# The gate's logits taken from TensorE's columns and given to GpSimd and VectorE

## The chip, the cores and the metric

The program runs on one core of a Trainium2 chip. A core has five engines with a program each, run in its own order: TensorE (matrix products; PE in the profile, its weight loads PEld), VectorE (DVE), ScalarE (ACT), GpSimd (POOL) and SyncE (SP), which here issues every DMA. An engine waits where an operand isn't ready; what stands behind the waiting instruction on that engine waits too. The metric is the device time of one execution in microseconds; lower is better.

## The reference

One input `x` of 2048 positions and 448 channels goes two ways, and a gate mixes the results:

```python
g = _sigmoid((x * gate_w).sum(-1, keepdims=True))
a = _A_ref(x, A_wqkv, A_wo)
b = _B_ref(x, B_w1, B_b1, B_w2, B_b2)
return g * a + (1 - g) * b
```

`_A_ref` makes q, k and v by one product `x @ wqkv`, lets every position look at 8 positions (itself and every second one before it, 16 heads of 28 channels), and multiplies by `wo`. `_B_ref` is a two-layer network, 448 to 1792 to 448, with the square of a relu between. Inputs and outputs are float32. The change concerns the first line: one number per position, the logit `z = sum over channels of x * gate_w`, whose sigmoid is `g`.

## The kernel before

**Products.** A float32 number is split into a high part of type `fp32r` and a low part, the rest, and a product is three: high by high, high by low, low by high. The high part is a ScalarE copy, the low part a VectorE subtraction, both in `split_full` (L113, L114). 448 channels are three full slices of 128 rows and one of 64. Nearly all products are written side by side (`side_by_side`, L187): two products of 64 rows each, in the upper and the lower half of the array, for two accumulators. An accumulator gets first one half of its rows, then the other; between the two, `turn` has one engine write to a spare element of it (L197: a VectorE memset of one element), so that the second half can't begin before the first is done.

**Chunks.** The positions come in four chunks of 512, each four tiles of 128. Of chunk 0, q is made slice by slice as the loads land (`qkv_first`, L258, whole-height products), then k and v in 36 and 42 pairs; chunks 1 to 3 are two calls of `qkv_two` each, for two tiles: 63 pairs, of which 24 begin q and k, 12 begin v, 18 end q and k, and 9 end v. Four x tiles of chunk c are split some microseconds before it starts; chunk 0's low parts (L659, L661, L114) are made at the very start, as its loads land. ScalarE moves a finished accumulator to SBUF (`qkv_evacuate`, L206), SyncE stores it to `q_d`, `k_d` or `v_d`.

**The gate.** The weights of q carry two more columns, `gate_w` twice, so q's accumulators have 450 columns, and their column 448 is the logit. A ScalarE copy of 128x1 (L214) puts it into `zt` after each of q's 16 tiles. `gates` makes the sigmoid of it at 126 µs.

**Order.** The program is one list, written in order of a model clock that counts TensorE's products: `when(t, ...)` and `at(dt, ...)` put a piece of work into the list when the model clock has come to a time, and each engine gets its instructions in the order of that list. `SPLIT_AT` has the times at which chunks are split. From chunk 2 on the attention (`qk_piece`, L334, and `av_piece`, L341) runs on GpSimd, each product of 128x896 followed by a VectorE reduction (L335, L349). GpSimd has nothing before that but a few memsets.

**Buffers.** Raw loads of x, of q's weights and of w1 share two buffers (`raw_tile`); a load waits until all readers of the tile before it have finished. The attention's products have four (`pp`), its logits two (`lg`).

SyncE's DMAs go into one queue each, in order; an instruction of SyncE that waits for a semaphore holds all DMAs behind it.

Of the kernel before, what the change touches and what calls it, by code (L numbers as in the profile page):

```python
# [7 lines left out]
F32 = mybir.dt.float32  # L8
F32R = mybir.dt.float32r
AF = mybir.ActivationFunctionType  # L10
ALU = mybir.AluOpType
AX = mybir.AxisListType

S, D, H, DH, W, F = 2048, 448, 16, 28, 8, 1792
P = 128
# [5 lines left out]
C = HG * DH  # L21
NF = F // P
CH = 512
NQ = D + 2
NP = 512


# [23 lines left out]
PP_BUFS = 4  # L51
# [5 lines left out]
def gated_mix_kernel(ctx: ExitStack, tc: tile.TileContext, xT, wqkv, w1, w2, wo, b1, b2, out):  # L57
    nc = tc.nc

    def f32(ap):  # L60
        return ap.bitcast(F32)
# [4 lines left out]
    k_d = tc.dram_tile([2, G, SP + HALO, C], F32, name="k_d")  # L66
    v_d = tc.dram_tile([2, G, SP + HALO, C], F32, name="v_d")
    x_d = tc.dram_tile([3, 4, P, 2, CH], F32, name="x_d")
    f_d = tc.dram_tile([2, NS, P, D], F32, name="f_d")


# [20 lines left out]
    smp = ctx.enter_context(tc.tile_pool(name="smp", bufs=2))  # L92
    prodp = ctx.enter_context(tc.tile_pool(name="prodp", bufs=1))
# [3 lines left out]
    zt, gt, g1t = zg[:, 0:2], zg[:, 2:4], zg[:, 4:6]  # L97
# [14 lines left out]
    def split_full(raw, hi, lo, soon=now):  # L112
        nc.scalar.activation(hi, raw, AF.Copy)  # L113
        soon(lambda: nc.vector.tensor_sub(lo, raw, f32(hi)))  # L114

    def split_x78(raw, x7, x8, soon=now):

        split_full(raw, x7, x8, soon)
# [32 lines left out]
    xcp = actx.enter_context(tc.tile_pool(name="phase_a_own", bufs=1, reuse_waits="tile"))  # L151
    wqh = ap.tile([P, 3, NP + 2 * D], F32R, name="wqh")
    wql = ap.tile([P, 3, NP + 2 * D], F32R, name="wql")

    w7h = ap.tile([P, NP + D], F32R, name="w7h")
    w7l = ap.tile([P, NP + D], F32R, name="w7l")
    ap.tile([P, 48], F32, name="pad_a")
# [3 lines left out]

    stage = {}

    def ncols(b):
        return NQ if b == 0 else D

    def block(b):

        o = (0, NP, NP + D)[b]
        return slice(o, o + ncols(b))  # L170

    class Acc:

# [26 lines left out]
    def qkv_evacuate(pt, c, tl, b):  # L200
        par, t = c // 2, (c % 2) * 4 + tl
        first = (b, t // 2) not in stage
        if first:
            stage[b, t // 2] = xap.tile([P, G, 2, C], F32, tag="stage", name=f"st{c}_{tl}_{b}", bufs=ST_BUFS)
        st = stage[b, t // 2]
        nc.scalar.activation(st[:, :, t % 2], pt[:, :D].rearrange("p (g c) -> p g c", g=G), AF.Copy)  # L206
        if not first:
            stage.pop((b, t // 2))
            t0 = t - t % 2
            dst, off = ((q_d, 0), (k_d, HALO), (v_d, HALO))[b]  # L210
            dd = dst[par, :, off:off + SP].rearrange("g (p s) c -> p g s c", s=NS)[:, :, t0:t0 + 2]
            nc.sync.dma_start(dd.rearrange("p g s c -> p g (s c)"), st.rearrange("p g s c -> p g (s c)"))
        if b == 0:
            nc.scalar.activation(zt[:, par, t:t + 1], pt[:, D:D + 1], AF.Copy)  # L214

    def full(x, acc, tl, b, ks=range(3)):
        sl, n = slice(tl * P, tl * P + P), block(b)
        r = []
        for k in ks:
            r += [(acc, x.h[k][:, sl], wqh[:, k, n]), (acc, x.h[k][:, sl], wql[:, k, n]),  # L220
                  (acc, x.l[k][:, sl], wqh[:, k, n])]
        return r

    def last(x, acc, tl, b):

        sl = slice(tl * P, tl * P + P)
        n = block(1) if b == 2 else slice(0, ncols(b))
        h, l = w7h[:, n], w7l[:, n]
        return [(acc, x.x7[:, sl], h), (acc, x.x7[:, sl], l), (acc, x.x8[:, sl], h)]

    def accs(c, b, tls, tags):
        return [Acc(t, f"qkv{c}_{tl}_{b}", ncols(b)) for t, tl in zip(tags, tls)]

    def run(c, todo, steps):

# [13 lines left out]
    def qkv_first(x):  # L249


        four = range(4)
        q = accs(0, 0, four, "bbbb")
        for k in range(3):
            for two in ((0, 1), (2, 3)):
                for j, prods in enumerate(zip(*(full(x, q[i], i, 0, (k,)) for i in two))):
                    for acc, a, w in prods:
                        nc.tensor.matmul(acc.pt[:, :NQ], a, w, start=k == j == 0, stop=False)  # L258
            advance(12 * MM448)
        for acc in q:  # L260
            acc.todo = 3
        k = accs(0, 1, four, "mmmm")
        t = [sum((last(x, a[i], i, b) for i in four), []) for b, a in ((0, q), (1, k))]
        f = [full(x, k[i], i, 1) for i in four]
        run(0, [t[0] + f[0] + f[1] + f[2] + f[3], t[1] + f[2] + f[3] + f[0] + f[1]],
            [(3, [(0, 0, q[0])], (k[0], k[0])),
             (12, [(0, i, q[i]) for i in (1, 2, 3)], (k[1], k[1])),
             (24, [], (k[0], k[2])), (33, [], (k[1], k[3])),
             (39, [(1, 0, k[0]), (1, 2, k[2])]), (48, [(1, 1, k[1]), (1, 3, k[3])])])
        v = accs(0, 2, four, "bbbb")  # L270
# [200 lines left out]
    def soon(fn):  # L471
        at(LO_DELAY, fn)

    def advance(dt):
        clock["pe"] += dt
        while due := [x for x in later if x[0] <= clock["pe"]]:
            item = min(due, key=lambda x: x[0])
            later.remove(item)
            item[1]()
        if not clock["on"]:  # L480
            clock["att"] = clock["pe"]
            return
# [12 lines left out]
    def raw_tile(name):  # L495
        return rawp.tile([P, 4, 512], F32, tag="raw", name=name)
# [134 lines left out]
    raws = [raw_tile("wqraw0")]  # L631
    rx = raw_tile("xraw0")
    for k in range(4):
        if k < 3:
            nc.sync.dma_start(raws[0][:, k, :NQ], wqkv[0, :, k])  # L635
        else:
            for b, rows in ((0, slice(0, 64)), (1, slice(64, P))):
                nc.sync.dma_start(raws[0][rows, k, :NQ], wqkv[b, rows, k])
        for cols in ((slice(0, 256), slice(256, CH)) if k == 0 else (slice(0, CH),)):
            nc.sync.dma_start(rx[:, k, cols], xT[0, :, k, cols])  # L640

    for b, tag in ((1, "k"), (2, "v")):
        raw = attp.tile([P, 3, D], F32, tag=tag, name=f"wqraw{b}")
# [4 lines left out]
    nc.sync.dma_start(raw7, wqkv[2, :, 3, :D])  # L648
    x = x_tiles(0, xap)
    for k in range(3):  # L650
        nc.scalar.activation(wqh[:, k, :NQ], raws[0][:, k, :NQ], AF.Copy)
        halves = (slice(0, 256), slice(256, CH))
        for i, cols in enumerate(halves):

            if k == i == 0:
                nc.vector.tensor_copy(x.h[k][:, cols], rx[:, k, cols])
            else:
                nc.scalar.activation(x.h[k][:, cols], rx[:, k, cols], AF.Copy)  # L658
        nc.vector.tensor_sub(wql[:, k, :NQ], raws[0][:, k, :NQ], f32(wqh[:, k, :NQ]))  # L659
        for cols in halves:  # L660
            nc.vector.tensor_sub(x.l[k][:, cols], rx[:, k, cols], f32(x.h[k][:, cols]))  # L661
    split_full(raws[0][:, 3, :NQ], w7h[:, :NQ], w7l[:, :NQ])
    split_x78(rx[:, 3], x.x7, x.x8)

    def wq_split(b, k):
        if k < 3:
            split_full(raws[b][:, k], wqh[:, k, block(b)], wql[:, k, block(b)])
        else:
            split_full(raw7, w7h[:, NP:], w7l[:, NP:])

    def when(t, fn, *args):
        later.append((t, lambda: fn(*args)))

    xs, xm = {0: x}, {}
    xraw = {1: x_load(1)}
# [30 lines left out]
        wq_split(1, k)  # L708
    for k in range(4):
        when(12000.0 + k * 900.0, wq_split, 2, k)  # L710
    for c, t in SPLIT_AT.items():
        when(t, x_begin, c)
        for k in range(4):
            when(t + k * 900.0, lambda c, k: x_split(xraw[c], xs[c], k), c, k)
        if c < 3:
            when(t + 4500.0, x_more, c + 1)
            when(t + 5000.0, lambda c: x_spill(c, xs[c]), c)
# [321 lines left out]
    c, x = ORDER[0], xm[3]  # L1039
# [8 lines left out]
    for g in range(2, 2 * NF):  # L1048
        i, f = g // (NF // 2), g % (NF // 2) * 2
        c = ORDER[i]  # L1050
# [118 lines left out]
```

## Time and profile before

| | |
|---|---|
| time, median of 3 runs | 415.12 µs (414.99 to 416.3) |
| profiled execution, span from the first to the last instruction | 412.7 µs |
| TensorE busy | 408.2 µs (99%) |
| VectorE, ScalarE, GpSimd busy | 255.7, 211.3, 268.5 µs |
| DMA moved | 73.76 MB, 179 GB/s |

The profile gives the span of the profiled execution; 2.4 µs lie between it and the median time, the part of a run before the first and after the last instruction. A row of the groups names line, engine, operation, output and inputs by the program's names, shapes, count, busy time and mean duration of one, then the engine's idle time ahead of them and what ended it. A row of the timeline has start, duration, and in brackets the idle time before. `64*128 64x448` is a product of 64 rows on 128 columns with 448 columns moved through.

### The profile page before, as it was taken

The numbers are of one execution on the slowest core, as the hardware profiler recorded it, in microseconds if no ns is written. First come the engines' busy times: TensorE is split into PE (matmuls) and PEld (weight loads), VectorE is DVE, ScalarE is ACT, GpSimd is POOL, SyncE is SP. The second block draws the span as 40 slices with busy tenths as digits, with TensorE's granted clock in tenths as the row PEclk, the third lists the DMA queues.
The fourth block names the chain that finished last, engine by engine and source line by source line (L and its number), as shares of the span: only waits on it lengthen the run. The fifth ranks groups of instructions, "written<-read, shape, count | busy, mean of one in ns | idle before, by whom it ended". The sixth has DMA issues, their size and how long they took to land.

```text
span 412.7 us, 9327 instructions
## 1 busy us (share of the span) xinstructions
PE 408.2 (99%) x3835; PEld 378.0 (92%) x3835; DVE 255.7 (62%) x404; ACT 211.3 (51%) x477; POOL 268.5 (65%) x167
## 2 busy tenths in 40 slices
PE   8999999999999999999999999999999999999997
PEld 7999999999999999888888888989898888888996
DVE  4520433276767766777656798879576677891354
ACT  4641656388765565444565535444653254346540
POOL 0000001955999999989989899999899977940000
DMA  7989999969362315555112649764146630168304
GB/s 226 380 324 326 268 393 299 335 213 311 101 235 104 128 42 218 209 184 152 29 58 95 228 160 270 197 146 149 27 163 186 229 129 2 45 177 132 96 0 180
DMA packets 65611, 73.76 MB, mean 179 GB/s; under 512 B 32352, under 2 KB 58528, under 8 KB 65184
## 3 DMA queue, kind: packets, MB, share of 16 engines
q1 hardware_dynamic: 65568, 73.16, 55.1%
q8 instruction: 30, 0.49, 0.5%
q14 instruction: 13, 0.11, 0.1%
HBM read 45.71 MB, written 28.25 MB: 179 GB/s over the span
## 4 chain that ended last, share of the span: by engine, by line
PE 97%; DMA 1%; SPq 0%; DVE 0%; ACT 0%; issue 0%
PE b L187 33%; PE h L187 32%; PE qkv L187 23%; PE a L187 7%; PE qkv L258 1%; DMA xraw<-xT 1%; PE a L943 1%; PE last L943 0%; SPq L640 0%; SPq L635 0%; DVE bt L822 0%; ACT x L658 0%; PE last L935 0%; PE a L935 0%
## 5 line engine op out<-in xcount | busy, mean ns | idle before, releaser
L334 POOL TENSOR_TENSOR qk<-q,k 128x896 f32<-128x896 f32 x64 | 135.1, 2137 | 84.8 <-DMA k<-k_d 76.4
L341 POOL TENSOR_TENSOR av<-lg,v 128x896 f32<-128x896 f32 x64 | 119.4, 1961 | 6.3 <-DVE lg L335 5.8
L187 PE MATMUL qkv<-wqh,x 64*128 64x448 f32 (+1 forms) x528 | 89.1, 361 | 0.0
L615 DVE TENSOR_TENSOR h<-h,h 128x512 fp32r<-128x512 f32 x56 | 38.4, 688 | 65.9 <-ACT h L618 65.5
L187 PEld LDWEIGHTS qkv<-wqh,x 64*128 64x128 f32 x528 | 72.2, 184 | 0.8
L187 PE MATMUL qkv<-wql,x 64*128 64x448 f32 (+1 forms) x264 | 72.2, 360 | 0.0
L187 PE MATMUL b<-w2ah,h 64*128 64x448 f32 x448 | 68.5, 359 | 0.0
L187 PE MATMUL b<-w2bh,h 64*128 64x448 f32 x448 | 67.8, 360 | 0.0
L335 DVE TENSOR_REDUCE lg<-qk 128x32 f32<-128x896 f32 x64 | 67.0, 1074 | 0.0
L349 DVE TENSOR_REDUCE o<-av 128x112 f32<-128x896 f32 x64 | 66.4, 1070 | 0.1
L616 ACT ACTIVATE h<-h,b1z 128x512 f32<-128x512 f32 x56 | 36.7, 655 | 43.6 <-PE h L187 43.6
L187 PEld LDWEIGHTS b<-w2ah,h 64*128 64x128 f32 x448 | 46.9, 184 | 2.8
L187 PEld LDWEIGHTS b<-w2bh,h 64*128 64x128 f32 x448 | 45.3, 184 | 3.2 <-ACT h L567 0.3
L187 PEld LDWEIGHTS qkv<-wql,x 64*128 64x128 f32 x264 | 44.5, 184 | 0.4
L187 PE MATMUL b<-w2al,h 64*128 64x448 f32 x224 | 44.3, 358 | 0.0
L187 PE MATMUL b<-w2bl,h 64*128 64x448 f32 x224 | 43.2, 358 | 0.0
L206 ACT ACTIVATE st<-qkv 128x448 f32<-128x448 f32 x48 | 24.3, 546 | 34.8 <-PE qkv L187 26.9
L617 ACT ACTIVATE h<-h 128x512 fp32r<-128x512 f32 x56 | 33.5, 598 | 1.7
L618 ACT ACTIVATE h<-h 128x512 f32<-128x512 f32 x56 | 33.3, 594 | 0.0
L187 PE MATMUL h<-x,w1h 64*128 64x512 f32 x168 | 32.8, 386 | 0.0
L567 ACT ACTIVATE h<-h 128x4 fp32r<-128x4 f32 (+1 forms) x35 | 7.2, 207 | 43.1 <-PE b L187 43.0
L187 PE MATMUL h<-x2b,w1h 64*128 64x512 f32 x168 | 28.2, 386 | 0.0
(145 smaller groups left out, 728.7 us busy)
## 6 DMA issues: line engine op xcount, KB each, us to landing
k<-k_d SPq DMA_DIRECT2D x8, 840.0 KB, 6.4
v<-v_d SPq DMA_DIRECT2D x8, 840.0 KB, 4.8
x_d<-x SPq DMA_DIRECT2D x11, 512.0 KB, 6.6
q_d<-st SPq DMA_DIRECT2D x8, 448.0 KB, 4.1
k_d<-st SPq DMA_DIRECT2D x8, 448.0 KB, 4.6
v_d<-st SPq DMA_DIRECT2D x8, 448.0 KB, 5.9
w1raw<-w SPq DMA_DIRECT2D x4, 896.0 KB, 9.2
q<-q_d SPq DMA_DIRECT2D x8, 448.0 KB, 3.6
```

What stands on the lines that cost most here:

```text
L187: nc.tensor.matmul(acc.pt[:, :acc.n], a[rows], w[rows], start=acc.todo == acc.all, stop=acc.todo == 1)
L206: nc.scalar.activation(st[:, :, t % 2], pt[:, :D].rearrange("p (g c) -> p g c", g=G), AF.Copy)
L258: nc.tensor.matmul(acc.pt[:, :NQ], a, w, start=k == j == 0, stop=False)
L334: nc.gpsimd.tensor_mul(pr, q[:, s:s + 1].to_broadcast([P, W, C]), k[:, s:s + W])
L335: pending.append(lambda: nc.vector.tensor_reduce(lg[:, s], pr.rearrange("p w (h d) -> p w h d", h=HG), axis=AX.X, op=ALU.add))
L341: nc.gpsimd.tensor_mul(pr.rearrange("p (h d) w -> p w h d", h=HG), lg[:, s][:, :, :, None].to_broadcast([P, W, HG, DH]), v[:, s:s + W].rea ...
L349: nc.vector.tensor_reduce(o[:, g * C:(g + 1) * C], pr, axis=AX.X, op=ALU.add)
L567: nc.scalar.activation(ap, f32(ap), AF.Copy)
L615: nc.vector.tensor_sub(hl, pt, f32(hh))
L616: ops += [lambda pt=pt, r=r: nc.scalar.activation(pt, pt, AF.Relu, bias=b1t[:, f + r:f + r + 1]), lambda pt=pt, hh=hh: nc.scalar.activatio ...
L617: lambda pt=pt, hh=hh: nc.scalar.activation(hh, pt, AF.Square),
L618: lambda pt=pt, r=r, low=low: (nc.scalar.activation(pt, pt, AF.Square), at(delays[r], low))]
```

## The change

`ncols` goes: q's accumulators have 448 columns like k's and v's, and the 16 ScalarE copies of L214 go. The load of the weights still brings the two gate columns. New are:

```diff
-        wqh[:, k, :NQ] ... wql[:, k, :NQ] ... acc.pt[:, :NQ]
+        wqh[:, k, :D]  ... wql[:, k, :D]  ... acc.pt[:, :D]
-        if b == 0:
-            nc.scalar.activation(zt[:, par, t:t + 1], pt[:, D:D + 1], AF.Copy)
...
+    zs = smp.tile([P, 3, NZ], F32, tag="lg", name="zs")
+    zu = xcp.tile([P, CH], F32, tag="zu", name="zu")
+    zm = prodp.tile([P, W * C], F32, tag="pp", name="zm", bufs=PP_BUFS)[:, :CH]
+    zpart, zall, gw = zs[:, 0], zs[:, 1], zs[:, 2, 0:4]
+    nc.gpsimd.tensor_copy(gw[:, 0:3], raws[0][:, 0:3, D:D + 1].rearrange("p k n -> p (k n)"))
+    nc.gpsimd.tensor_copy(gw[0:64, 3:4], raws[0][0:64, 3, D:D + 1])
+
+    def z_products(raw):
+        for k in range(4):
+            r = slice(0, P if k < 3 else 64)
+            out = zm if k else zu
+            nc.gpsimd.tensor_mul(out[r], raw[r, k], gw[r, k:k + 1].to_broadcast([r.stop, CH]))
+            if k:
+                nc.gpsimd.tensor_add(zu[r], zu[r], zm[r])
+
+    def z_sums(c):
+        nc.vector.transpose(zu, zu)
+        nc.vector.tensor_reduce(
+            zpart.rearrange("p (b c t) -> p c t b", b=4, c=4)[:, c],
+            zu.rearrange("p (t b r) -> p t b r", t=4, b=4), axis=AX.X, op=ALU.add)
+
+    def z_move():
+        nc.sync.dma_start(z_d, zpart)
+        for b in range(4):
+            nc.sync.dma_start(
+                zall[b * 32:b * 32 + 32].rearrange("p (a n) -> p a n", a=4),
+                z_d[:, b * 16:b * 16 + 16].rearrange("(a c) n -> c a n", a=4))
+
+    def z_last():
+        nc.vector.tensor_reduce(
+            zt.rearrange("p q s -> p (q s)"), zall.rearrange("p (a n) -> p n a", a=4), axis=AX.X, op=ALU.add)
...
+    z_products(rx)
+    for c, t in enumerate((16500.0, 27000.0, 40000.0, 54500.0)):
+        when(t, z_sums, c)
+        if c < 3:
+            when(t + (500.0, 500.0, 5500.0)[c], lambda c: z_products(xraw[c + 1]), c)
+    when(59500.0, z_move)
+    when(67500.0, z_last)
```

For each chunk `z_products` has GpSimd multiply the raw x of a slice, channels on partitions and positions along the row, by the gate's weights and add up the slices: four products and three sums, 128x512 or 64x512, in one chain over `zu`. `z_sums` has VectorE transpose 32x32 blocks of `zu` in place, so that positions lie on partitions, and add up 32 channels. One tile `zu` serves all chunks, so the products of a chunk wait for the sums of the one before. Each of four groups of 32 partitions then has a part of each sum: `z_move` stores them to DRAM and reads them back in four DMAs with a group's parts beside each other, and `z_last` adds the four.

Four facts on the order of the engines. On VectorE, the sums of chunk 0 stand behind the last low part of the weights of v and ahead of the low parts of x of chunk 1 and the memsets that turn v's accumulators of chunk 0; the sums of chunk 3 stand ahead of the low part of x slice 2 and of the memset that turns the first accumulators of chunk 2; `z_last` stands ahead of the memsets that turn those of chunk 2's second half. On SyncE, `z_move` stands behind the first load of the attention's v and ahead of the stores of chunk 2. On GpSimd, the configuration instruction that the program has ahead of the first tensor_tensor stood behind the memsets; it now stands between the copies of the gate's weights and the first product.

More of the change, by code (lines that the diff above doesn't have):

```diff
@@ L24 @@
 NQ = D + 2
+NZ = 64
 NP = 512
@@ L68, in gated_mix_kernel @@
     x_d = tc.dram_tile([3, 4, P, 2, CH], F32, name="x_d")
+    z_d = tc.dram_tile([P, NZ], F32, name="z_d")
     f_d = tc.dram_tile([2, NS, P, D], F32, name="f_d")
@@ L162, in gated_mix_kernel @@
     stage = {}
-    def ncols(b):
-        return NQ if b == 0 else D
     def block(b):
         o = (0, NP, NP + D)[b]
-        return slice(o, o + ncols(b))
+        return slice(o, o + D)
     class Acc:
@@ L226, in last @@
         sl = slice(tl * P, tl * P + P)
-        n = block(1) if b == 2 else slice(0, ncols(b))
+        n = block(1) if b == 2 else slice(0, D)
         h, l = w7h[:, n], w7l[:, n]
@@ L231, in accs @@
     def accs(c, b, tls, tags):
-        return [Acc(t, f"qkv{c}_{tl}_{b}", ncols(b)) for t, tl in zip(tags, tls)]
+        return [Acc(t, f"qkv{c}_{tl}_{b}", D) for t, tl in zip(tags, tls)]
     def run(c, todo, steps):
@@ L257, in qkv_first @@
                     for acc, a, w in prods:
-                        nc.tensor.matmul(acc.pt[:, :NQ], a, w, start=k == j == 0, stop=False)
+                        nc.tensor.matmul(acc.pt[:, :D], a, w, start=k == j == 0, stop=False)
             advance(12 * MM448)
@@ L650, in gated_mix_kernel @@
     for k in range(3):
-        nc.scalar.activation(wqh[:, k, :NQ], raws[0][:, k, :NQ], AF.Copy)
+        nc.scalar.activation(wqh[:, k, :D], raws[0][:, k, :D], AF.Copy)
         halves = (slice(0, 256), slice(256, CH))
@@ L658, in gated_mix_kernel @@
                 nc.scalar.activation(x.h[k][:, cols], rx[:, k, cols], AF.Copy)
-        nc.vector.tensor_sub(wql[:, k, :NQ], raws[0][:, k, :NQ], f32(wqh[:, k, :NQ]))
+        nc.vector.tensor_sub(wql[:, k, :D], raws[0][:, k, :D], f32(wqh[:, k, :D]))
         for cols in halves:
             nc.vector.tensor_sub(x.l[k][:, cols], rx[:, k, cols], f32(x.h[k][:, cols]))
-    split_full(raws[0][:, 3, :NQ], w7h[:, :NQ], w7l[:, :NQ])
+    split_full(raws[0][:, 3, :D], w7h[:, :D], w7l[:, :D])
     split_x78(rx[:, 3], x.x7, x.x8)
+    zs = smp.tile([P, 3, NZ], F32, tag="lg", name="zs")
[25 more added lines that the diff above has]
+            zt.rearrange("p q s -> p (q s)"), zall.rearrange("p (a n) -> p n a", a=4), axis=AX.X, op=ALU.add)
     def wq_split(b, k):
```

## The prediction

> **What bounds the kernel now.** I read the page's busy shares and slices first, then the chain that ended last, then the groups by shape.
>
> ```profile
> span 412.7 us, 9327 instructions
> PE 408.2 (99%) x3835; PEld 378.0 (92%) x3835; DVE 255.7 (62%) x404; ACT 211.3 (51%) x477; POOL 268.5 (65%) x167
> ...
> POOL 0000001955999999989989899999899977940000
> DMA  7989999969362315555112649764146630168304
> ...
> PE 97%; DMA 1%; SPq 0%; DVE 0%; ACT 0%; issue 0%
> ```
>
> TensorE is busy 99% of the span and makes 97% of the chain that ended last: what TensorE does less is gained, and what makes it wait is lost, whole. GpSimd is empty for the first 70 µs, just where the new work goes; the DMA engines are full there (9 in most of the first eight slices).
>
> **The gain: narrower products.**
>
> ```profile
> L187 PE MATMUL qkv<-wqh,x 64*128 64x448 f32 x384 | 81.0, 359 | 0.0
> L187 PE MATMUL qkv<-wqh,x 64*128 64x450 f32 x144 | 44.1, 364 | 0.0
> ```
>
> ```profile
> 51.02 0.39 PE L187 MATMUL qkv<-wqh,x 64*128 64x448 f32 x2
> ...
> 51.25 0.53 PE L187 MATMUL qkv<-wqh,x 64*128 64x450 f32 x2
> ...
> 53.42 0.47 PE L187 MATMUL qkv<-wqh,x 64*128 64x448 f32 x2
> ...
> 53.73 0.45 PE L187 MATMUL qkv<-wqh,x 64*128 64x450 f32 x2
> ```
>
> The means differ by 5 ns. The pace shows more: in one stretch of pairs, from 51.02 to 53.42 the row half with 448 columns starts 12 products in 2.40 µs, 200 ns each; from 51.25 to 53.73 the half with 450 takes 2.48, 206.7 ns. Two columns cost 6.7 ns. The 24 pairs at the start of each of six half-chunks go at q's pace: 6 x 24 x 6.7 ns = 0.96 µs. Bounds: 0.2 (where only one half is slow, the other may set the pace in part) and 1.0; I take 0.9, since these 24 pairs come as two runs with q in the same half. The whole-height products of chunk 0 are paced by loads and splits: nothing. The 16 small copies of L214 go from ScalarE, which is idle half of the span, and no product waits for them: nothing.
>
> **The new work on GpSimd.** 28 products and sums, two small copies.
>
> ```profile
> L334 POOL TENSOR_TENSOR qk<-q,k 128x896 f32<-128x896 f32 x64 | 135.1, 2137 | 84.8 <-DMA k<-k_d 76.4 <-DVE lg L335 5.4 <-DVE o L349 2.3
> L387 POOL TENSOR_TENSOR lg<-lg,sm 128x256 f32<-128x256 f32 x8 | 5.1, 636 | 2.3 <-ACT h L618 2.3
> L349 DVE TENSOR_REDUCE o<-av 128x112 f32<-128x896 f32 x64 | 66.4, 1070 | 0.1
> L352 DVE STREAM_TRANSPOSE o<-o 128x448 f32<-128x448 f32 x16 | 10.2, 638 | 0.3
> L114 DVE TENSOR_TENSOR x<-xraw,x 128x512 fp32r<-128x512 f32 x13 | 8.4, 690 | 14.1 <-ACT x L113 14.1
> ```
>
> Between 256 elements (636 ns) and 896 (2137) lies 512 at 636 + 256 x 2.345 = 1236 ns. A chunk's seven are one chain over `zu`: 8.7 µs; four chunks 34.6 µs, which the idle 69.8 µs can hold. VectorE's sums: transposition 638 x 512/448 = 730, reduction 1070 x 512/896 = 610, with the hand-over 1.4 µs a chunk. So the amount fits; what counts is who stands behind a late step.
>
> **When the first chain can begin.**
>
> ```profile
> 0.74 1.28 ACT L651 ACT_TABLE_LOAD   x1 [0.74 <-PEq L1161]
> ```
>
> ```profile
> wqraw<-wqkv SPq DMA_DIRECT2D x2, 112.5 KB, 5.5
> ```
>
> ```profile
> 4.03 1.20 SPq L638 DMA_DIRECT2D wqraw<-wqkv  x2
> ```
>
> The second copy of the gate's weights waits for the first half of slice 3, issued at 4.03 and landing 5.5 µs later (rows two and three): 9.6. Then comes the configuration instruction. Before, it ran at 1.3 with GpSimd's first product at 71.2, so its price doesn't show. Its nearest rows: ScalarE's table load, 1.28 µs, and, if code comes through the same full queues, a transfer of that moment, 5.5 µs. I take 5.5: a table is loaded ahead of any traffic, this comes amid it. The first product starts at about 15.2.
>
> [...]
>
> **Who shares with whom.** While the chain of chunk 0 runs, VectorE makes low parts with two SBUF operands:
>
> ```profile
> 16.59 0.63 DVE L114 TENSOR_TENSOR wql<-wqraw,wqh 128x448 fp32r<-128x448 f32 x1 [2.99 <-ACT wqh L113]
> 17.32 0.09 DVE L197 MEMSET qkv<- 1x1 f32 x2
> 17.41 1.16 DVE L114 TENSOR_TENSOR wql<-wqraw,wqh 128x448 fp32r<-128x448 f32 x2
> 19.12 0.09 DVE L197 MEMSET qkv<- 1x1 f32 x2 [0.55 <-PE qkv L187]
> 19.21 0.62 DVE L114 TENSOR_TENSOR w7l<-wqraw,w7h 128x448 fp32r<-128x448 f32 x1
> 24.23 1.93 DVE L114 TENSOR_TENSOR x<-xraw,x 128x512 fp32r<-128x512 f32 x3 [4.40 <-ACT x L113]
> 25.52 0.06 DVE L197 MEMSET qkv<- 1x1 f32 x2
> ...
> 27.52 0.09 DVE L197 MEMSET qkv<- 1x1 f32 x2 [0.75 <-PE qkv L187]
> ```
>
> ```profile
> 71.19 12.58 POOL L334 TENSOR_TENSOR qk<-q,k 128x896 f32<-128x896 f32 x6 [69.80 <-DMA k<-k_d]
> ```
>
> ```profile
> L335 DVE TENSOR_REDUCE lg<-qk 128x32 f32<-128x896 f32 x64 | 67.0, 1074 | 0.0
> ...
> L513 ACT ACTIVATE copy<-w1raw 128x448 f32<-128x448 f32 x8 | 4.4, 548 | 2.0 <-DVE w1l L518 1.1 <-DVE w17l L518 0.8
> ```
>
> No such subtraction ever runs beside a GpSimd product in this trace: those of L114 are over before its first product at 71.19, and from there each VectorE subtraction has a PSUM operand (L518 from `copy`, L615 from `h`). So the price is open: nothing, or turns, where each subtraction waits for the product under way (up to 1.24 µs) and the next product for it (0.62 to 0.69). For nothing speaks that L335, with one SBUF operand, takes 1.07 µs beside GpSimd and without it; but it is of another kind. For turns speaks that every subtraction after 71 µs comes with a ScalarE copy of its operand to PSUM (L513, 548 ns), work that no number needs if two SBUF operands cost nothing there. I take turns, at three to one.
>
> [...]
>
> **The sum, stage by stage.** Chain 0 starts at 15.2, needs 8.7, and gives way to four subtractions (16.59 to 19.83, 4 x 0.62 = 2.5): it ends at 26.4. VectorE, in its order, now does chunk 0's sums (27.8), and only then what it did from 24.23 on. By then chain 1 is free to run, so: subtraction 0.69, product 1.24, subtraction 0.69, memset 0.1: 30.5. Product, subtraction, product, subtraction (3.9), memset: 34.4. These memsets turn v's accumulators; when TensorE needs them shows in its rows:
>
> ```profile
> 27.23 0.43 PE L187 MATMUL qkv<-wqh,x 64*128 64x448 f32 x2
> ...
> 63.39 0.36 PE L187 MATMUL qkv<-wqh,x 64*128 64x450 f32 x1
> ...
> 76.15 0.37 PE L187 MATMUL qkv<-wqh,x 64*128 64x450 f32 x1
> ```
>
> v's second half starts at 27.23 (after 24 of its 42 pairs), the other two tiles 9 pairs later, 29.0. TensorE waits 3.3 µs for the first and 5.4 in all for the second. Slack covered these steps, 1.6 and 1.4 µs (25.58 to 27.23, 27.61 to 29.03); without it TensorE stays late.
>
> Later sums: chain 1 ends about 39 and its sums at 40.4, ahead of a need at 38.1 + 5.4. Chain 2 ends at 49, its sums stand behind work of 45.1 + 5.4. Chain 3 waits for x of chunk 3:
>
> ```profile
> xraw<-xT SPq DMA_DIRECT2D x1, 1024.0 KB, 7.0
> ```
>
> ```profile
> 58.34 2.54 DVE L114 TENSOR_TENSOR x<-xraw,x 128x512 fp32r<-128x512 f32 x4 [5.84 <-ACT x L113]
> 60.24 0.06 DVE L197 MEMSET qkv<- 1x1 f32 x2
> ```
>
> ```profile
> 65.47 0.32 SPq L315 DMA_DIRECT2D v<-v_d  x1
> ```
>
> ```profile
> 56.20:81.70 25.50, 25.50 (x255) 24.73 (x254) 8.02 (x25) 13.74 (x30) 10.51 (x6) 1.00 1.00 334
> ```
>
> ```profile
> o_d<-o SPq DMA_DIRECT2D x16, 224.0 KB, 2.2
> ...
> ot<-o_d SPq DMA_DIRECT2D x16, 32.0 KB, 2.6
> ```
>
> Its load, issued at 46.2, lands at 53.2; the chain then takes 8.7 and two turns (1.4) to 63.3, sums 64.7, one subtraction and a memset 65.5. TensorE needs that at 63.39: 2.1 late in the old timing. The move: its store is queued behind v's load of 840 KB, issued at 65.47, itself behind k's, which lands at 71.1 (the row of GpSimd above); at the 334 GB/s of that stretch (last column of the row by stretches) v lands at 73.7. SyncE waits for the store, then issues four loads (0.4 each); they land 2.6 µs later (32 KB of `ot`), z_last ends about 78.5, the need is 76.15: 2.4 late. Both are counted against TensorE's old time: a TensorE 5.4 late, with the full DMA queues draining during its wait, meets both. They add nothing; without the first stall they would be the bound. GpSimd's attention starts at 71 or later, long after the chains; SyncE's stores of chunk 2 wait up to 6 µs behind the move, and ScalarE needs their buffers at 78.6 or later.
>
> Sum: + 5.4 - 0.9 = + 4.5 µs: a span of 417.2, and with the same 2.4 around it 419.6. The page gives no time of that execution beside its span; I take it to stand at the median.
>
> **The rivals.**
> - The configuration is short, 1.3 µs, with turns. The chain starts at 11.0 and meets chunk 0's own low parts: k's weights of slices 1 and 2 come about 0.8 and 1.9 late, then the memset at 19.12 comes at 24.1 for a need at 20.6; 3.5 lost in all, x's low parts then are in time. 415.1 + 3.5 - 0.9 = 417.7. Against it: the rows of loads at that moment.
> - No turns. The chain ends at 23.9, sums 25.3, the memset 26.8 for a need at 27.23: nothing lost there. Then z_move's 2.4 decides, with 0.7 of chain 3 (61.9 + 1.4 + 0.8 for 63.39) inside it: + 2.4 - 0.9, 416.6. For it: every VectorE row beside GpSimd is unslowed.
> - On the other side: the whole path of the logits is hidden, 415.1 - 0.9 = 414.2. One condition decides, that z's five DMAs don't queue behind v: if the store lands in the 2.2 µs of an `o_d` store, at 68, z_last is done by 73, before 76.15. It needs no turns as well. Against it: in the rows of the full stretch each load lands in order, 5 to 7 µs after issue.
> - VectorE gets its turn only when the chain ends: every low part behind 23.9 instead of 17.2, then again 8.7 µs of chain 1 ahead of x's low parts: 27.8 after the sums, 36.5 after chain 1, 39.3 for a need at 29.0, 10.3 lost: 424.5.
>
> **How the numbers follow.** Forecast 419.6: 0.53. Short configuration, 417.7: 0.13. No turns, 416.6: 0.18. Hidden: 0.05. No turn at all for VectorE, or longer configuration amid the traffic: 0.11. A measurement tells 0.3%, 1.25 µs, from no change. Faster by more than that: 0.02. Within it (up to 416.4): most of the hidden case and two fifths of the no-turns case, 0.11. Slower: 0.87. The range runs from 416.2 to 422.6: the lower end takes in the no-turns case, the upper a chain 3 µs later; the likeliest case alone has 418.3 (turns half as long) to 421.
>
> **What would show it.** In the changed profile: q's pairs at 200 ns; GpSimd's first product not before 15, with no row in the gap; VectorE's L114 rows beside it over 1 µs or started late, at gaps ended by GpSimd; a wait of TensorE near 29 to 34 on a VectorE memset, about 5 µs together, and none near 63 to 82. It is wrong if the chain begins by 11, if subtractions beside products start at once, or if TensorE's waits stand at z_last instead.

## The result and the profile after

The changed kernel takes 418.89 µs, median of 6 runs (418.25 to 423.62), beside 415.0 µs before on the same chip (414.19 to 416.3): a ratio of 1.0119, 95% interval 1.0082 to 1.0156. The profiled run took 418.62 µs with a span of 416.8, where before has a span of 412.7. In the changed file the line numbers have moved: L116 makes low parts, L186 is the side-by-side product, L196 the memset that turns an accumulator, L674 GpSimd's products, L676 its sums, L680 and L681 VectorE's transposition and sum.

The page of after:

```profile
span 416.8 us, 9352 instructions
...
PE 409.2 (98%) x3835; PEld 365.3 (88%) x3835; DVE 271.6 (65%) x413; ACT 210.7 (51%) x461; POOL 304.7 (73%) x197
...
POOL 1878152863999999989989999999989977940000
```

TensorE's busy time is hardly changed, and less than the span by more than before. GpSimd now works in the first seven slices. TensorE's waits up to 90 µs in after, each at the product that it ends at (timeline: start, duration, in brackets the wait and what ended it; a smaller loss near 94.5 follows below):

```profile
14.43 0.67 PE L186 MATMUL qkv<-w7h,x 64*128 64x448 f32 x4 [1.02 <-DVE x L116]
18.83 0.47 PE L186 MATMUL qkv<-wql,x 64*128 64x448 f32 x2 [0.50 <-DVE wql L116]
32.30 0.47 PE L186 MATMUL qkv<-wqh,x 64*128 64x448 f32 x2 [0.80 <-DVE qkv L196]
67.54 0.47 PE L186 MATMUL qkv<-wqh,x 64*128 64x448 f32 x2 [0.76 <-DVE qkv L196]
```

Before, TensorE has no wait in this stretch. All the waits are for VectorE, none for GpSimd: GpSimd acts through VectorE. To put sizes on it I take the stages of TensorE, from the start of one group of pairs to the next, worked out from the starts of its products in each trace. For all kernels of this study, in µs:

```
                    chunk 0   chunk 1   chunk 2 (a)  chunk 2 (b)  chunk 3 (a)   span
before               18.12     25.39      12.76        12.76        12.87      412.7
after                21.48     25.20      13.64        12.60        13.00      416.8
e1 narrow only       18.12     25.20      12.60        12.60        12.68      412.4
e2 memsets           19.55     25.20      14.35        12.60        12.69      414.9
e3 late chain 0      19.21     25.87      17.03        13.24        12.68      418.8
e4 tail moved        24.08     25.20      12.60        12.60        12.68      418.3
e5 both moves        19.20     25.87      12.60        12.60        12.68      414.9
e6 one operand       18.12     25.20      18.81        12.60        12.68      418.2
e7 on VectorE        18.12     25.20      12.60        12.60        12.67      412.0
e8 e6 and e4         18.12     25.20      12.60        12.60        12.67      412.4
```

Against the undisturbed stages (row e1) the changed kernel loses 3.36 µs in chunk 0, 1.04 in the first half of chunk 2 and 0.32 in the first half of chunk 3, 4.72 in all. Before is 0.70 longer than row e1 in these stages, so the difference is 4.02, of 4.1 between the spans. The stages leave out where the pairs begin, which moves from execution to execution: 12.4 to 13.2 µs in these ten traces, 12.71 in before and 13.20 in e1. That is why e1's span is only 0.3 below before's; spans that lie a few tenths apart should not be compared.

**The start.** GpSimd and VectorE in after, the same stretch (start, duration):

```profile
9.60 0.18 POOL L667 COPY zs<-wqraw 64x1 f32<-64x1 f32 x1 [1.33 <-DMA xraw<-xT]
9.82 1.22 POOL L674 TENSOR_TENSOR zu<-xraw,zs 128x512 f32<-128x512 f32 x1
...
13.91 1.37 POOL L674 TENSOR_TENSOR zm<-xraw,zs 128x512 f32<-128x512 f32 x1
15.36 1.56 POOL L676 TENSOR_TENSOR zu<-zu,zm 128x512 f32<-128x512 f32 x1
...
24.60 1.04 POOL L674 TENSOR_TENSOR zm<-xraw,zs 128x512 f32<-128x512 f32 x1
25.72 1.31 POOL L676 TENSOR_TENSOR zu<-zu,zm 128x512 f32<-128x512 f32 x1
```

```profile
12.62 1.76 DVE L116 TENSOR_TENSOR x<-xraw,x 128x512 fp32r<-128x512 f32 x1
14.30 6.68 DVE L116 TENSOR_TENSOR wql<-wqraw,wqh 128x448 fp32r<-128x448 f32 x5
...
20.91 0.61 DVE L116 TENSOR_TENSOR wql<-wqraw,wqh 128x448 fp32r<-128x448 f32 x1
...
26.48 4.24 DVE L116 TENSOR_TENSOR x<-xraw,x 128x512 fp32r<-128x512 f32 x3 [3.02 <-ACT x L115]
...
30.65 1.52 DVE L116 TENSOR_TENSOR x<-xraw,x 128x512 fp32r<-128x512 f32 x1
```

The first product stands 0.04 µs behind the copy. From then on five subtractions of 128x448 take 6.68 µs, 1.34 each on average: by single instructions 1.46, 1.72, 1.46 and 1.71 beside the chain, and 0.64 for the fifth, which starts behind the chain's end at 19.92. The one at 20.91, with GpSimd idle too, takes 0.61. GpSimd is slowed less: a product of 1.04 alone takes up to 1.37, a sum of 1.31 up to 1.62. The stage of chunk 0 has three groups of pairs, with 12, 36 and 42: they start at 12.74, 16.55 and 24.75 and the next stage at 34.22, so they lose 1.30, 0.99 and 1.07 µs against 12 x 0.210, 36 x 0.200 and 42 x 0.200 in row e1.

**The tail.** VectorE in after near 66, then SyncE and VectorE near 75:

```profile
65.38 0.71 DVE L680 STREAM_TRANSPOSE zu<-zu 128x512 f32<-128x512 f32 x1 [1.18 <-POOL zu L676]
66.12 0.69 DVE L681 TENSOR_REDUCE zs<-zu 128x16 f32<-128x512 f32 x1
66.73 1.32 DVE L116 TENSOR_TENSOR x<-xraw,x 128x512 fp32r<-128x512 f32 x2
67.40 0.71 DVE L196 MEMSET qkv<- 1x1 f32 x5
```

```profile
69.38 0.33 SPq L687 DMA_DIRECT2D z_d<-zs  x1
76.70 1.75 SPq L689 DMA_DIRECT2D zs<-z_d  x4
...
80.51 2.61 SPq L523 DMA_DIRECT2D w1raw<-w  x2
```

```profile
79.74 0.27 DVE L695 TENSOR_REDUCE zg<-zs 128x16 f32<-128x64 f32 x1 [5.70 <-DMA zs<-z_d]
```

VectorE stands 1.18 µs before chunk 3's transposition, and the memset behind it, which TensorE needed at 66.6, comes at 67.40. SyncE stands 6.9 µs for the store of the logits; z_last ends at 80.01, in time for the memsets behind it (needed at 80.26), but the loads of w1 behind it are issued at 80.51 (71.19 before), and the chain that ended last runs from that load (to 87.12) by ScalarE and VectorE to a memset at 94.81; TensorE's next pair starts behind it at 94.94, 0.2 µs late.

### The profile page after: what moved, and what is told of

It is laid out like the page before. It is cut to its first block, busy times and chain, and to the rows that moved or that the text cites. A ratio compares the mean times of both kernels' runs of the same rounds, so it can differ in the third digit from the quotient of the medians.

```text
span 416.8 us, 9352 instructions
## 1 busy us (share of the span) xinstructions
PE 409.2 (98%) x3835; PEld 365.3 (88%) x3835; DVE 271.6 (65%) x413; ACT 210.7 (51%) x461; POOL 304.7 (73%) x197
## 4 chain that ended last, share of the span: by engine, by line
PE 84%; DMA 8%; DVE 3%; issue 2%; SPq 1%; ACT 1%; DVEq 0%
PE b L186 32%; PE h L186 32%; PE qkv L186 12%; PE a L186 7%; DMA v_d<-st 2%; DMA z_d<-zs 2%; DMA w1raw<-w 2%; DMA wqraw<-wqkv 1%; DVE wql L116 1%; DVE x L116 1%; DMA xraw<-xT 1%; PE a L983 1%; DVE lg L332 1%; ACT st L205 0%; SPq L211 0%
## 5 line engine op out<-in xcount | busy, mean ns | idle before, releaser
L612 DVE TENSOR_TENSOR h<-h,h 128x512 fp32r<-128x512 f32 x56 | 38.4, 688 | 66.9 <-ACT h L615 66.6
L186 PE MATMUL qkv<-wqh,x 64*128 64x448 f32 x528 | 78.6, 360 | 1.6 <-DVE qkv L196 1.6
L186 PE MATMUL b<-w2ah,h 64*128 64x448 f32 x448 | 66.3, 359 | 0.0
L186 PE MATMUL b<-w2bh,h 64*128 64x448 f32 x448 | 66.2, 360 | 0.0
L186 PEld LDWEIGHTS qkv<-wqh,x 64*128 64x128 f32 x528 | 49.4, 184 | 6.2 <-DVE qkv L196 2.7
L186 PE MATMUL qkv<-wql,x 64*128 64x448 f32 x264 | 48.1, 361 | 0.5 <-DVE wql L116 0.5
L186 PEld LDWEIGHTS b<-w2bh,h 64*128 64x128 f32 x448 | 42.0, 184 | 3.8 <-ACT h L564 0.3
L186 PEld LDWEIGHTS b<-w2ah,h 64*128 64x128 f32 x448 | 41.9, 184 | 3.7
L186 PE MATMUL b<-w2bl,h 64*128 64x448 f32 x224 | 40.7, 358 | 0.0
L186 PE MATMUL b<-w2al,h 64*128 64x448 f32 x224 | 40.5, 358 | 0.0
L186 PE MATMUL h<-x,w1h 64*128 64x512 f32 x168 | 28.2, 386 | 0.0
L186 PE MATMUL h<-x0b,w1h 64*128 64x512 f32 x168 | 28.1, 386 | 0.0
L186 PE MATMUL h<-x1b,w1h 64*128 64x512 f32 x168 | 28.1, 386 | 0.0
```

The costliest lines, as they stand in the source:

```text
L186: nc.tensor.matmul(acc.pt[:, :acc.n], a[rows], w[rows], start=acc.todo == acc.all, stop=acc.todo == 1)
L612: nc.vector.tensor_sub(hl, pt, f32(hh))
```

## The experiments

My theory after the result: VectorE's subtractions with two operands in SBUF are slowed beside GpSimd's work (chunk 0), and the places of the late sums and of the move in the queues cost the rest; the narrower products by themselves gain something under 1 µs. Rivals: the narrow products gain nothing; any work of GpSimd slows VectorE; the tail's waits are covered anyway.

**e1_narrow: the gain alone.**

```diff
-    zs = smp.tile([P, 3, NZ], F32, tag="lg", name="zs")
...
+    nc.gpsimd.memset(zt, 0.0)
...
-    z_products(rx)
...
-    when(59500.0, z_move)
-    when(67500.0, z_last)
```

> Only the narrow products: q's products with 448 columns as in the changed kernel, and no work on the gate's logits at all (their tile is set to zero, so the gate is 0.5 everywhere: the logits are left out). This measures the gain of the change by itself. My theory: the four row-tiled products of q's last 64 channels pace 200 ns a pair instead of 206.7, so 6 pairs x 24 tiles x 6.7 ns = 0.96 us less than before, 0.9 to 1.0, time 414.0 to 414.2 on a median of 415.0 before; no gap in TensorE between 12.7 and 34, the two-SBUF-operand subtractions of VectorE at 0.6 to 0.7 us each as before, chunk 0's stage 18.0 us. Rival, that the narrow products are worth nothing, since TensorE waits for the splits of weights and x at the same times anyway: 414.8 to 415.2. Rival, that the start of the changed kernel is late for another reason than GpSimd's work (the narrower splits, another order of the queues): 417 to 418.5, the same gaps near 13 to 19 us as in the changed kernel.

413.62 µs (11 runs) beside 414.5 before: ratio 0.998, interval 0.9971 to 0.9989, or 0.88 µs, a little under the 0.9 to 1.0 expected (whose 6 x 24 stands for six half-chunks of 24 pairs, as in the prediction). No wait of TensorE in the stretch, the subtractions at 0.61 to 0.70. The change itself gains. In the stages it is 0.70: 0.16 to 0.19 in three of the six half-chunks; the two of chunk 1 give 0.19 together, and the last gives none. Nothing here shows where the other 0.18 of the 0.88 lie; the interval, 0.5 to 1.2 µs, takes in both.

**e2_writes: GpSimd works, but only writes.**

```diff
-    z_products(rx)
+    for k in range(7):
+        for _ in range(3):
+            nc.gpsimd.memset(zm if k in (1, 3, 5) else zu, 0.0)
```

> The changed kernel, but GpSimd's seven products and sums of chunk 0 are replaced by 21 memsets of the same two tiles, which only write (so chunk 0's logits are left out, the sums of chunks 1 to 3 are as in the changed kernel). My theory, that VectorE's subtractions with two operands in SBUF are slowed by GpSimd's operations that read SBUF: beside memsets the subtractions of wql and x take 0.62 to 0.7 us again instead of 1.34 to 1.76, the gaps of TensorE between 13 and 19 us are gone, chunk 0's stage is 21.5 - 2.3 = 19.2 us with the 1.1 us at 31 us left (x of chunk 1 beside chunk 1's products), and the time is about 2.3 us under the changed kernel, 416.3 to 416.9. Rival, that any work of GpSimd on SBUF slows VectorE: the subtractions stay at 1.3 us or more for as long as the memsets run, and the time stays within 0.5 us of the changed kernel, 418.4 to 419.4.

417.04 µs, ratio 1.0074 (1.0048 to 1.01), 0.1 above the range expected. The larger of GpSimd's two groups from 9 to 22 µs, then VectorE's timeline of e2:

```profile
L746 POOL MEMSET zu<- 128x512 f32 x12 | 6.3, 526 | 0.5
```

```profile
11.19 0.69 DVE L116 TENSOR_TENSOR x<-xraw,x 128x512 fp32r<-128x512 f32 x1 [0.24 <-ACT x L115]
11.80 1.76 DVE L116 TENSOR_TENSOR wql<-wqraw,wqh 128x448 fp32r<-128x448 f32 x3
...
23.92 4.36 DVE L116 TENSOR_TENSOR x<-xraw,x 128x512 fp32r<-128x512 f32 x3 [1.47 <-ACT x L115]
```

GpSimd is busy without a pause, and the subtractions take what they took before: 0.69, and 1.76 for three. At 23.92, beside the real chain of chunk 1, they take 1.45 each again, and chunk 0 keeps 1.43 µs of its loss. So it isn't GpSimd's work as such: memsets, which only write, cost VectorE nothing. With the start repaired TensorE comes earlier to chunk 2 and meets chunk 3's sums at the same old place: that stage loses 1.75 instead of 1.04. Part of the gain, 0.7 µs, was given back there.

**e3_late0: chunk 0's chain moved behind the weights' low parts.**

```diff
+    def gw_late():
+        nc.vector.tensor_copy(gw[:, 0:3], gw0[:, 0:3])
...
-    z_products(rx)
+    when(15000.0, gw_late)
+    when(15100.0, z_products, rx)
-    for c, t in enumerate((16500.0, 27000.0, 40000.0, 54500.0)):
+    for c, t in enumerate((22300.0, 34300.0, 43500.0, 54500.0)):
...
-            when(t + (500.0, 500.0, 5500.0)[c], lambda c: z_products(xraw[c + 1]), c)
+            when(t + 500.0, lambda c: z_products(xraw[c + 1]), c)
```

> The changed kernel with chunk 0's seven GpSimd operations held back until VectorE has done the last split of v's weights (VectorE hands over the gate's four weights by a copy there), so about 20 to 29 us instead of 10 to 20, and the sums of chunks 0 to 2 moved behind that. All the work remains. My theory: the start's loss of 2.3 us (gaps of TensorE at 13.0, 17.1 and 18.0) and most of the 1.1 us at 31.1 go, chunk 0's stage is 18.0 to 18.4 us, while the gap at 66.4 (chunk 3's sums ahead of a memset that a turn waits for, 0.9 us) and the one at 94.5 (0.3) stay: 3.1 to 3.4 us under the changed kernel, 415.5 to 415.9. Rival, that the contention only moves with the chain, since x of chunk 1 is split at 26 to 32 us beside it: chunk 0's stage stays above 19.5 us, time 417 to 418.5.

420.57 µs, ratio 1.0149 (1.0135 to 1.0163): no gain on the changed kernel, whose interval (1.0082 to 1.0156) overlaps this one, and my expectation was off by 5 µs. In the traces the span is 2.0 longer. Chunk 0 came to 19.21, between the 18.0 to 18.4 expected and the rival's 19.5: x of chunk 1 is now split beside the chain, as the rival had it. Chunk 1 lost 0.67, as low parts ahead of a memset now met the chain of chunk 2; chunk 2 lost 4.43 and 0.64, the first at one place:

```profile
64.72 0.37 PE L186 MATMUL qkv<-w7h,x 64*128 64x448 f32 x2
67.84 0.74 PE L186 MATMUL qkv<-wqh,x 64*128 64x448 f32 x2 [2.76 <-DVE qkv L196]
68.38 0.58 PE L186 MATMUL qkv<-wql,x 64*128 64x448 f32 x2
...
70.62 0.49 PE L186 MATMUL qkv<-wql,x 64*128 64x448 f32 x2
```

This is the wait of 67.5 in after, grown to 2.76 µs since TensorE is earlier and chunk 3's chain later; and behind it the pairs start 0.373 µs apart up to 70.6 instead of 0.200.

The 0.64 show the contention at its plainest. TensorE being late, low parts of w1 fell beside the attention's products. VectorE and GpSimd in e3 (the groups from 74 to 84 µs, then the timeline), and the same low part in the groups of before, from a ScalarE copy of w1 in PSUM (L518) and from SBUF (L114):

```profile
L116 DVE TENSOR_TENSOR w17l<-w1raw,w17h 64x128 fp32r<-64x128 f32 x3 | 6.3, 2117 | 0.1
```

```profile
73.51 8.52 POOL L331 TENSOR_TENSOR qk<-q,k 128x896 f32<-128x896 f32 x4 [7.87 <-DMA k<-k_d]
```

```profile
L518 DVE TENSOR_TENSOR w17l<-copy,w17h 64x128 fp32r<-64x128 f32 x6 | 1.7, 291 | 0.1
L114 DVE TENSOR_TENSOR w17l<-w1raw,w17h 64x128 fp32r<-64x128 f32 x6 | 1.7, 286 | 0.3
```

A subtraction of 0.29 µs takes 2.12, as long as one product (8.52 / 4 = 2.13): it ends only when the product does. With its first operand in PSUM the same subtraction keeps its 0.29, in a time in which GpSimd multiplies as well.

**e4_tail: only the tail moved.**

```diff
-    for c, t in enumerate((16500.0, 27000.0, 40000.0, 54500.0)):
+    for c, t in enumerate((16500.0, 27000.0, 40000.0, 60000.0)):
-    when(59500.0, z_move)
-    when(67500.0, z_last)
+    when(78500.0, z_move)
+    when(86000.0, z_last)
```

> The changed kernel with only the tail of the logits' work moved: the sums of chunk 3 come behind the memsets of chunk 2's last turns (model time 60.0 instead of 54.5), the move of the logits through DRAM 19 us later (78.5 instead of 59.5), its last sum at 86.0 instead of 67.5. The start is left as it is. My theory: the gap of TensorE at 66.4 (0.9 us) and the one at 94.5 (0.3 us, from the loads of w1 that SP issued 9.3 us later) go, stage 3 and the 20 us behind it are as before: 1.2 to 1.3 us under the changed kernel, 417.5 to 417.8. Rival, that both are covered by later waits (TensorE is behind ACT or VectorE there in any case): 418.6 to 419.1. Rival, that the moved store and loads now hold up SP's later loads: the time is above 419.1.

418.07 µs, median of 4 runs from 416.83 to 420.12, ratio 1.0092 (1.0065 to 1.0119): 0.3 above the expected range, but four runs that lie 3.3 µs apart decide nothing. The stages answer: chunk 2 12.60 and chunk 3 12.68, both losses of the tail are gone, so they were real. The profiled execution (420.12) isn't a clean one at the start: chunk 0 took 24.08. TensorE's windows in e4 (from:to, length, busy times; then the granted clock, DMA share, GB/s):

```profile
13.10:16.10 3.00, 1.47 (x7) 0.87 (x8) 3.00 (x3) 0.00 (x0) 2.84 (x3) 0.81 0.48 129
16.10:21.40 5.30, 5.30 (x32) 4.71 (x30) 4.68 (x4) 3.48 (x9) 3.42 (x3) 0.50 0.70 266
```

After a stretch in which TensorE was busy half of the time, its clock was at half for 5.3 µs; 15 pairs at 0.373 µs instead of 0.200 cost 2.6, which is what chunk 0 lost beyond the 21.48 of after. The three faster runs weren't traced.

**e5_both: both moves.** The edits of e3 and e4 together.

> Both moves together: chunk 0's GpSimd work held back as in e3_late0, the tail moved as in e4_tail. My theory of e3's loss: it was not the start (chunk 0's stage 19.2 us, 2.3 us under the changed kernel) but chunk 3's sums standing ahead of the memset that TensorE waits for, at 64.7 (3.1 us, and 1.5 us more in pairs that pace 373 ns right behind it), and the last sum of the logits at 81.8 (0.5). With the tail moved both go: 418.8 - 4.4 - 0.6 is a span of 413.8, 415.3 to 416.2 in time; the gaps at 28.7 (1.2, x of chunk 1 beside GpSimd) and near 51 (0.7) stay. Rival, that e3's late chunk 3 has its cause in the raw x of chunk 3 (loaded only when chunk 2's chain has let go of the buffer): then TensorE waits for chunk 3's x near 66 to 70 whatever the order, 417.5 or more.

417.1 µs (416.73 to 417.48), ratio 1.0064. The stages of chunks 2 and 3 are clean, as expected: e3's 5 µs there came from the places of the tail's steps, not from chunk 3's x, which is loaded as in e3. But the time is 0.9 above the expected range. One wait is new, of TensorE in e5, and SyncE's timeline has its cause:

```profile
110.93 0.49 PE L186 MATMUL h<-x,w1h 64*128 64x512 f32 x2 [1.15 <-ACT w1h L564]
```

```profile
84.37 1.24 SPq L691 DMA_DIRECT2D z_d<-zs  x1
90.66 1.75 SPq L693 DMA_DIRECT2D zs<-z_d  x4
92.51 0.39 SPq L551 DMA_DIRECT2D w2raw<-w  x1
```

The store of the logits held SyncE for 5 µs here too, now in front of w2's loads; ScalarE's and VectorE's work on w2 then stands in front of the copy that TensorE waits for. In e7 and e8 the same move comes 1.3 µs earlier or so, and two pairs near 108 µs are 0.2 to 0.3 longer together.

**e6_ptr: products that read one tensor.**

```diff
-            nc.gpsimd.tensor_mul(out[r], raw[r, k], gw[r, k:k + 1].to_broadcast([r.stop, CH]))
+            nc.gpsimd.tensor_scalar(out[r], raw[r, k], gw[r, k:k + 1], None, op0=ALU.mult)
```

> The changed kernel with the 16 products written as a multiplication by a scalar of each partition, so that a product reads one tensor from SBUF and not two (the gate's weight as a broadcast operand); the 12 sums still read two. Nothing else is moved. My theory, that any GpSimd operation which reads a tensor from SBUF contends with VectorE's subtractions: those beside products still take 1.2 us or more, the start's gaps stay, and the time moves only by what shorter products give, 417.6 to 419.0. Rival, that it takes two operands on both sides: the subtractions beside products are back at 0.62 to 0.69, only those beside the sums are slowed, so 3 of 7 steps contend, chunk 0's stage is 19.0 to 20.5 us instead of 21.5, and the time 416.3 to 417.5.

420.55 µs, ratio 1.0149 (1.013 to 1.0168), so by time alone both theories fail. The trace says more. GpSimd, VectorE and TensorE in e6:

```profile
11.73 2.10 POOL L674 TENSOR_SCALAR zm<-xraw,zs 128x512 f32<-128x512 f32 x1
...
15.32 1.57 POOL L674 TENSOR_SCALAR zm<-xraw,zs 128x512 f32<-128x512 f32 x1
16.97 1.31 POOL L676 TENSOR_TENSOR zu<-zu,zm 128x512 f32<-128x512 f32 x1
...
25.22 2.28 POOL L674 TENSOR_SCALAR zm<-xraw,zs 128x512 f32<-128x512 f32 x1
```

```profile
11.27 0.68 DVE L116 TENSOR_TENSOR x<-xraw,x 128x512 fp32r<-128x512 f32 x1
11.87 2.10 DVE L116 TENSOR_TENSOR wql<-wqraw,wqh 128x448 fp32r<-128x448 f32 x3
...
17.27 2.02 DVE L116 TENSOR_TENSOR wql<-wqraw,wqh 128x448 fp32r<-128x448 f32 x2
...
26.08 1.08 DVE L116 TENSOR_TENSOR x<-xraw,x 128x512 fp32r<-128x512 f32 x1
```

```profile
67.89 0.74 PE L186 MATMUL qkv<-wqh,x 64*128 64x448 f32 x2 [4.56 <-DVE qkv L196]
```

Beside a product that reads one tensor most subtractions are back at 0.61 to 0.70. In several products one subtraction still loses 0.4 µs: of the three at 11.87 the middle one takes 1.03, and the one at 26.08 takes 1.08. These products grow, from 1.57 to between 2.10 and 2.40. The subtraction at 17.27, which meets a sum, takes 1.49, as in the changed kernel. Chunk 0 is at 18.12: the whole 3.36 is gone. My theory, that any reading contends alike, is wrong. The rival is nearer, though chunk 0 came out under its 19.0 to 20.5 and the time over its 416.3 to 417.5: a VectorE subtraction waits for a whole GpSimd instruction where both read two tensors, and loses little beside this one. The edit changes the kind of instruction together with the number of tensors that it reads; which of the two decides isn't separated here.

All of it and more was lost again at one place. A product of one operand takes 1.57 alone, 0.5 longer; chunk 3's chain takes 11.4 µs instead of 9.1 and ends at 65.68 (65.34 in after) though it begins 2 µs earlier. TensorE comes there 3.5 µs earlier than in after, and the memset behind the sums costs it a wait of 4.56 µs and a slow clock for some 7 pairs behind it.

**e7_vec: the products on VectorE.**

```diff
-            nc.gpsimd.tensor_mul(out[r], raw[r, k], gw[r, k:k + 1].to_broadcast([r.stop, CH]))
-            if k:
-                nc.gpsimd.tensor_add(zu[r], zu[r], zm[r])
+        if k:
+            nc.vector.scalar_tensor_tensor(zu[r], raw[r, k], gw[r, k:k + 1], zu[r], op0=ALU.mult, op1=ALU.add)
+        else:
+            nc.vector.tensor_scalar(zu, raw[:, k], gw[:, k:k + 1], None, op0=ALU.mult)
...
+    for c, (t, gap) in enumerate(((14800.0, 300.0), (22300.0, 600.0), (37800.0, 450.0), (60000.0, 600.0))):
...
+    when(78500.0, z_move)
+    when(86000.0, z_last)
```

> The logits by VectorE alone: for each slice one operation that multiplies x by the gate's weight of each partition and adds what is there (4 instead of 7 a chunk), then the same transposition and sums, put into VectorE's idle stretches (chunk 0 behind the last low part of v's weights, chunks 1 to 3 behind x's low parts and the turns), the tail as in e4_tail; GpSimd only copies the gate's weights. My theory, that the change itself is right (0.9 us by narrower products, measured alone) and that all of the loss comes from GpSimd beside VectorE and from the places in the queues: no subtraction is slowed, chunk 0's stage is 18.0 to 18.3 us, no gap in TensorE but the one at 13, and the time 0.6 to 0.9 us under before. Rival, that VectorE has not the time, about 4 us a chunk by the subtractions' rows of 0.62 to 0.69 for an operation: its memsets come late at v's turns of chunk 0 (26 to 31 us) or at chunk 1, and the time is 0.3 to 2 us above before.

413.8 µs (11 runs) beside 414.37: ratio 0.9987, interval 0.9979 to 0.9996. VectorE in e7:

```profile
18.87 0.63 DVE L116 TENSOR_TENSOR w7l<-wqraw,w7h 128x448 fp32r<-128x448 f32 x1
19.42 0.48 DVE L674 TENSOR_SCALAR zu<-xraw,zs 128x512 f32<-128x512 f32 x1
19.93 2.39 DVE L672 SCALAR_TENSOR_TENSOR zu<-xraw,zs,zu 128x512 f32<-128x512 f32 x3
...
23.10 0.69 DVE L679 TENSOR_REDUCE zs<-zu 128x16 f32<-128x512 f32 x1
23.89 1.93 DVE L116 TENSOR_TENSOR x<-xraw,x 128x512 fp32r<-128x512 f32 x3
```

One chunk takes VectorE 4.4 µs, from 19.42 to 23.8, and fits between the last low part of the weights and the first of x: no subtraction is slowed and no stage of the table is longer than in e1. The time is 0.6 under before, at the edge of the 0.6 to 0.9 expected; 0.25 µs go to the two pairs near 108 µs. This version beats both kernels, by 0.6 µs against before and, by the ratios, by 1.3% against the changed one.

**e8_ptr_tail: both repairs on GpSimd.** The edits of e6 and e4 together.

> The two repairs that each took away one part of the loss, in one kernel, with all the work still on GpSimd: products that read one tensor from SBUF (as in e6_ptr) and the tail moved (as in e4_tail). My theory, that the loss of the changed kernel is these two places and nothing else: chunk 0's stage is 18.1 us as in e6_ptr, the gap at 63 to 68 us (4.9 us, and 1.4 us of slow pairs behind it) is gone, so 418.2 - 6.2 is a span of 412.0, 413.6 to 414.6 in time, under or at the time before. Rival, that GpSimd's longer chain of chunk 3 (54 to 66 us instead of 55 to 64) holds TensorE by another way (its raw x is released late, or chunk 2's sums stand ahead of a memset near 45 to 52): a gap of TensorE between 45 and 75 us remains and the time is 415 or more. Rival, that the moved transfers hold SP's loads of w2 as in e5_both (1.3 us of wait at 109.4): 414.8 to 415.6.

414.43 µs (11 runs from 413.71 to 416.29) beside 414.54: ratio 1.0, interval 0.9988 to 1.0012. The stages of the table are those of e1 and the span is 412.4, near the 412.0 expected. So in the traced execution the two places account for the whole loss up to 100 µs: with another form of the products and the tail in another place, GpSimd does all the work at no cost to TensorE there, and 0.3 µs go to the two pairs near 108 µs. By the median the loss isn't wholly gone: e1 and e7 gain on before, e8 doesn't, and its single runs go up to 416.29. Where the slower ones lose their time wasn't traced.

## Why the prediction was right, and where its steps were not

The forecast of 419.6 (416.2 to 422.6) holds 418.89, and slower was right. The span was put at 417.2 and is 416.8; the rest is what lies around it, 1.8 µs here and not the 2.4 that I took from the median before: in every run, of before too, the time exceeds the span by 1.7 to 2.3 µs, mostly 1.8, so the profiled execution of before, at 412.7, stood below that median. But the sum was made of terms of which two are wrong, and their errors go opposite ways.

- **"I take 5.5" for the configuration instruction: failed.** The nearest rows, a table load and a transfer of that moment, were both wrong for it: the first product starts at 9.82, 0.04 µs after the copy, and the two rows of the configuration itself (9.7 and 9.8) take 4 ns each. By the prediction's own words ("It is wrong if the chain begins by 11") the likeliest case failed here.
- **The place and size of the first stall: failed with it.** I put 5.4 µs at v's turns. It was 3.36: 2.29 at the low parts of x and of the weights between 13 and 19 µs, 1.07 at v's turn. That is the first rival, the short configuration with turns, which had 0.13. Its 3.5 agrees with 3.36 in part by luck: it had the loss at the memset that turns k's accumulators and x's low parts of chunk 1 in time, while the waits came at chunk 0's own low parts and then at v's turn, behind x's. Its time, 417.7, lacks the tail's 1.36.
- **Turns: confirmed.** They were an estimate: no row of before has such a subtraction beside a product. One subtraction goes by for about each product or sum, 0.8 to 1.1 µs longer (1.46 to 1.76); the product grows by 0.2 to 0.3, not by the 0.62 that I added for each turn. The row of 2.12 µs for a subtraction of 0.29 in e3 shows the wait for a whole product, and the argument from the copies to PSUM held. But it goes for instructions with two tensors on both sides; memsets (e2) don't do it (0.69, and 1.76 for three subtractions, as before), and the products of e6, which read a single tensor, do it little: neither blocks for the whole of the other. At most one subtraction in a product loses 0.4 µs, and that product grows by 0.5 to 0.8.
- **"They add nothing" for the later sums: failed.** The 2.1 µs that I worked out for chunk 3 in the old timing were to vanish in a stall of 5.4. The stall was 3.36 at the start of chunk 1, chunk 3's load landed later too (the chain began at 56.28, where I had 53.2), and 1.04 were left. z_move held SyncE as worked out, and z_last was in time by 0.2 µs; that the loads of w1 stand behind the move, and cost 0.32 at 94.5, I didn't see: the prediction named the stores behind it only. The sign "none near 63 to 82" failed at 67.5 with it.
- **The gain: 0.9 taken, 0.70 by the stages, 0.88 by the times of e1 (0.5 to 1.2 by the interval).** The pace of 200 ns came as forecast; the last half-chunk and half of chunk 1 gave nothing.
- **GpSimd's durations.** 1.24 forecast; 1.04 for a product whose second operand is broadcast, 1.30 for a sum, a chain alone takes 8.4 (chunk 2's, 34.91 to 43.3), forecast 8.7. VectorE's sums 1.4, as measured.

In sum: 4.5 was forecast as 5.4 + 0 - 0.9 and came as 3.36 + 1.36 - 0.70, which is 4.02. What held is the mechanism of turns between VectorE and GpSimd that reach TensorE through VectorE's queue. That the number came within 0.5 is partly luck: the start was put 2.0 too high, the tail 1.4 too low.

## What to carry to other kernels

An idle engine is not a free one: before moving work to GpSimd, list what VectorE does beside it with two operands in SBUF, and price each of them at one whole GpSimd instruction more at worst when that reads two tensors as well (0.29 became 2.12 here, 0.61 became 1.46 to 1.72); the same work on VectorE itself, in a gap that fits, was cheaper. A step placed in an in-order queue holds what stands behind it (SyncE's for 6.9 µs in after), so a repair that makes the bounding engine earlier makes the next such place dearer: of what they had gained at chunk 0, e2 lost a part at chunk 3's sums, and e3 and e6 lost more than all. Repair all of them before judging one by time, and read stages, not totals.

## What the runs showed of the hardware that was not expected

- **A wait can cost more than its length.** Behind waits of 2.76 µs (e3) and 4.56 µs (e6), and behind a stretch half idle (e4), pairs started 0.373 µs apart for 3 to 6 µs. The single waits of 1.5 µs or less in after (up to 1.02), e2 (1.5) and e5 (1.15) left the pace as it was. TensorE's row in e6 from 64 to 71 µs, with the wait in it, has a granted clock of 0.76 (the third number from the end):

```profile
64.00:71.00 7.00, 3.12 (x18) 2.79 (x20) 3.78 (x12) 0.00 (x0) 2.28 (x3) 0.76 0.87 296
```

  In e4 no single wait was longer than 1.0 µs, so the length of one wait alone doesn't decide; what does isn't shown here.
- **The form of a GpSimd product counts:** 1.57 µs as a multiplication by a scalar of each partition, 1.04 with that scalar as a broadcast tensor, all 128x512 and alone; a sum of two full tensors takes 1.30.
- **VectorE's products** of 128x512: 0.48 µs by a scalar alone, 0.75 with the sum in the same instruction.
